# Two score items of the second attention block side by side: four unsplit matmuls in one run on TensorE

## The chip, the core and the metric

The kernel runs on one core of a Trainium2 chip. The metric is device time in microseconds (us) of one execution, as the median of several runs. Before the change three runs gave 736.40, 738.48 and 741.03 us.

## The reference

Attention with a window, then a gated feed-forward. There are 4 batches, 8 heads, 768 positions and 64 dimensions a head. A query sees the 96 positions up to itself (`n_local`) and the first 8 positions (`n_global`); a slope per head times the distance is subtracted from its score.

```
scores = scale * q @ k.T + bias                # bias = -slope[h] * dist
scores = where(is_global | is_local, scores, -1e9)
a = exp(scores - max(scores)); a = a / (sum(a) + 1e-9)
x = (a @ v) reshaped to 3072 x 512
out = (sigmoid(x @ w_gate) * (x @ w_val)) @ w_out   # 512 -> 1536 -> 512
```

Everything is float32.

## The kernel before

**Blocks and units.** The 3072 tokens are cut into 8 blocks of 384 (three tiles of 128). A block's feed-forward is 12 units, one for each slice f of 128 of the 1536 inner features. Unit (block, f) is `ff_in` (L554: 12 matmuls for the gate into bank `ps_g`, 12 for the value into `ps_u`; tanh of the gate on ScalarE, L572; the product on VectorE, L578 or L581) and one unit later `ff_out` (L588: into `ps_o0` to `ps_o2`). Most feed-forward products are made of three matmuls, each on a high or a low part of its two operands ("split").

**Attention of a block** is done in 12 items, (s, t): head pair s of 4, token tile t of 3. For one item:

- `scores` (L359, event "S"): each head of the pair is one matmul with a contraction of 64, on rows 0 to 63 or 64 to 127 of the array. In blocks 0 and 1 (`PAIR` = 1) the float32 operands are used unsplit (L373), head j in bank j; from block 2 on they are split and use the whole array (L387). VectorE then adds the bias table and finds the row minimum of the negated scores (L406), ScalarE takes the exponential (L419). The results go to a buffer of tag `work`, of which there are four; the gate's tanh uses the same tag.
- `normalise` and `transposes` (event "T"): in block 1 VectorE divides by the row sums (L436, L438), TensorE transposes into bank `ps_t` (L452) and ScalarE copies it out (L457).
- `values` (event "V", once per head pair): a @ v into bank `ps_t` (L502), then `pair_out` (L515) splits the result into `xh` (L544) and `xl` (L545), the operands of the next block's `ff_in`.

Block 1's attention runs inside the 12 feed-forward units of block 0. Its scores use two banks, `ps_s` and `ps_v`; each item takes both, so an item's matmuls wait until VectorE has read the item before. Item k of block 1 has its S at unit k*10//12, T and V one unit later.

**Weights.** In the same units the weights are converted from float64 words, slice by slice: DMA on SyncE's queue (`raw`, L175 and L177), ScalarE (L192, L199, and `w1h` at L235), VectorE (L201 to L214), GpSimd (`w1l`, L180). `ff_in` of slice f needs `w1h` and `w1l` of f. From f = 6 on, and in all later blocks, `ff_out` needs `w2h` (ScalarE, L217) and `w2l` (GpSimd, L180).

**Order.** The code gives each unit's events in four groups: 0 ahead of `ff_in`, 1 after its gate matmuls, 2 after `ff_in`, 3 after `ff_out`. This is the order in which instructions are written down, which is their precedence; the framework then simulates the program with its own cost model and lays down, for each engine and for each DMA queue, a fixed order of what it found ready. On the chip each engine goes through its list in that order. `issue_after` adds an edge that fixes an order on an engine.

Of the kernel before, what the change touches and what calls it, by code (L numbers as in the profile page):

```python
# [15 lines left out]
ALU = mybir.AluOpType  # L16
# [3 lines left out]
P = 128  # L20
PREV = 96
GLOB = 32
SLOT = GLOB + P
WIN = PREV + SLOT
# [4 lines left out]
def attn_moe_kernel(ctx, tc, qT, kT, v, n_global, n_local, wg, wv, wo, out, B, H, S, D):  # L29
    nc = tc.nc  # L30
# [28 lines left out]
    wraw = cstack.enter_context(tc.tile_pool(name="wraw", bufs=1))  # L59
    late = {}  # L60

    def issue_after(later, earlier):
        tc.add_manual_dep(
            later.ins,
            earlier.ins.name,
            mybir.DependencyInfo(mybir.DependencyClass.NoSync, mybir.DependencyReason.DATA),
            reason="issue order",
        )

# [22 lines left out]
    last_pe = []  # L92
# [54 lines left out]
    last_min = []  # L147
# [120 lines left out]
    PAIR = 1  # L268
    blocks = [(b, t0, TB) for b in range(B) for t0 in range(0, NTB, TB)]
# [14 lines left out]
    steps = {}  # L284
# [66 lines left out]
    def bank(*names):  # L351

        i = turns.get(names, 0)
        turns[names] = i + 1
        name = names[i % len(names)]
        pool = {"ps_s": ps_a, "ps_t": ps_a, "ps_v": ps_a, "ps_g": ps_gv, "ps_u": ps_gv}.get(name, ps_o)
        return pool.tile([P, 4 * P], F32, name=name)

    def scores(bi, s, t):  # L359
        b, t0, nt = blocks[bi]  # L360
        st = steps[bi, s]
        zero = t0 + t == 0
        w = P if zero else WIN
        qc = slice(t * P, (t + 1) * P)
        k0 = t * SLOT + WIN - w
        if bi <= PAIR:

            ps = [bank(*(("ps_s", "ps_g", "ps_u", "ps_o1") if bi < PAIR else ("ps_s", "ps_v"))) for _ in range(2)]

            lead = None  # L370
            for j in (1, 0):
                hd = slice(j * D, (j + 1) * D)
                ins = nc.tensor.matmul(  # L373
                    ps[j][:, :w], st["qr"][hd, 0, qc], st["kr"][hd, k0:k0 + w], start=True, stop=True
                )
                if lead is not None:
                    issue_after(ins, lead)
                lead = ins
            last_pe[:] = [lead]
            if (bi, s, t) == (0, 0, 1):  # L380
                keep_busy(4)
        else:
            both = bank("ps_s")
            ps = [both[:, j * WIN:(j + 1) * WIN] for j in range(2)]
            for j in range(2):
                for hl in (1, 0):
                    nc.tensor.matmul(  # L387
                        ps[j][:, :w],
                        st["qs"][:, j, hl, qc],
                        st["ks"][:, j, k0:k0 + w],  # L390
                        start=(hl == 1),
                        stop=(hl == 0),
                    )
        build_pair(s, zero, dist)
        sb = mpool.tile([P, 2, WIN], F32, name="work", tag="work", bufs=WORKB)
        i = 2 * ((b * NTB + t0 + t) * NPAIR + s)
        nm = nms[:, i:i + 2]
        if bi < PAIR:
            if t == 0:
                st["sums"] = small.tile([P, 2 * nt], F32, name="sums", bufs=2)  # L400
            sm = st["sums"][:, 2 * t:2 * t + 2]
        else:
            sm = small.tile([P, 2], F32, name="sm")
        for j in range(2):

            ins = nc.vector.tensor_tensor_reduce(  # L406
                sb[:, j, :w],
                ps[j][:, :w],
                (tabs0 if zero else tabs)[2 * s + j],
                -SCALE,  # L410
                3.0e38,
                op0=ALU.add,
                op1=ALU.min,
                accum_out=nm[:, j:j + 1],
            )
            if j and bi <= PAIR:
                issue_after(ins, last_min[-1])
            last_min[:] = [ins]
            ins = nc.scalar.activation(  # L419
                sb[:, j, :w], sb[:, j, :w], AF.Exp, scale=-1.0, bias=nm[:, j:j + 1], accum_out=sm[:, j:j + 1]  # L420
            )
            last_exp[:] = [ins]
        st["s", t] = (sb, sm)
# [91 lines left out]
    def pair_out(bi, s, av, st):  # L515
        b, t0, nt = blocks[bi]
        n = nt * P
        xh, xl = x_of(bi)
        if bi < PAIR:

            sm = st["sums"]
            nc.vector.tensor_scalar(sm, sm, 1e-9, None, op0=ALU.add)
            rc = small.tile([P, 2 * nt], F32, name="rcs", bufs=2)
            nc.vector.reciprocal(rc, sm)
            rows = ps_o.tile([P, 4 * P], F32, name="ps_o2")
            for t in range(nt):
                for j in range(2):
                    nc.tensor.matmul(
                        rows[j * D:(j + 1) * D, t * P:(t + 1) * P],
                        rc[:, 2 * t + j:2 * t + j + 1].to_broadcast([P, D]),  # L530
                        ident,
                        start=True,
                        stop=True,
                    )
            rs = mpool.tile([P, NB], F32, name="hl", tag="hl")
            nc.scalar.copy(rs[:, :n], rows[:, :n])
            x = mpool.tile([P, NB], F32, name="hh", tag="hh")
            nc.vector.tensor_tensor(x[:, :n], av[:, :n], rs[:, :n], op=ALU.mult)
            if s < NPAIR - 1:
                nc.gpsimd.tensor_copy(xh[:, s, :n], x[:, :n])  # L540
                sub(nc.gpsimd, xl[:, s, :n], x[:, :n], xh[:, s, :n])
                return
            av = x
        nc.scalar.activation(xh[:, s, :n], av[:, :n], AF.Copy)  # L544
        nc.vector.tensor_tensor(xl[:, s, :n], av[:, :n], xh[:, s, :n], op=ALU.subtract)  # L545
# [4 lines left out]
    last_out = []  # L550
# [3 lines left out]
    def ff_in(bi, f, mid=None):  # L554
        b, t0, nt = blocks[bi]
        n = nt * P
        xh, xl = x_of(bi)
        pss = []
        for i in range(2):
            ps = ps_gv.tile([P, NB], F32, name=("ps_g", "ps_u")[i])  # L560
            k = 0
            for c in range(NC):
                for wt, xt in ((w1l, xh), (w1h, xl), (w1h, xh)):
                    nc.tensor.matmul(  # L564
                        ps[:, :n], wt[f][:, i, c], xt[:, c, :n], start=(k == 0), stop=(k == 3 * NC - 1)
                    )
                    k += 1
            pss.append(ps)
            if i == 0:
                a = mpool.tile([P, NB], F32, name="work", tag="work", bufs=WORKB)  # L570

                last_gate[:] = [nc.scalar.activation(a[:, :n], ps[:, :n], AF.Tanh, scale=0.5)]  # L572
                if mid is not None:
                    mid()
        if bi < PAIR and f < UNSPLIT:

            h = mpool.tile([P, NB], F32, name="hh", tag="hh")
            nc.vector.scalar_tensor_tensor(h[:, :n], a[:, :n], 1.0, pss[1][:, :n], op0=ALU.add, op1=ALU.mult)  # L578
            hs[bi, f] = (h,)
            return  # L580
        nc.vector.scalar_tensor_tensor(a[:, :n], a[:, :n], 1.0, pss[1][:, :n], op0=ALU.add, op1=ALU.mult)  # L581
        hh = mpool.tile([P, NB], F32R, name="hh", tag="hh")
        hl = mpool.tile([P, NB], F32R, name="hl", tag="hl")
        nc.scalar.activation(hh[:, :n], a[:, :n], AF.Copy)  # L584
        sub(nc.vector, hl[:, :n], a[:, :n], hh[:, :n])
        hs[bi, f] = (hh, hl)
# [45 lines left out]
    events = []  # L632
    for bi, (b, t0, nt) in enumerate(blocks):
        items = [(s, t) for s in range(NPAIR) for t in range(nt)]
        if bi < PAIR:
            w = (-200, -80)
        elif bi == PAIR:
            w = (0, NF - LEAD)
        else:

            w = ((bi - 1) * NF - (LEAD + 1 if bi > PAIR + 1 else 0), bi * NF - LEAD - 1)
        for k, (s, t) in enumerate(items):
            u = w[0] + k * (w[1] - w[0]) // len(items)

            lag = AHEAD if bi < PAIR else 1
            events.append((u, 0, "S", bi, s, t))
            events.append((u + lag, 1, "T", bi, s, t))
            if bi > PAIR:
                events.append((u + 2 * lag, 1, "J", bi, s, t))
            if t == nt - 1:  # L650
                after, kind = (2, 2) if bi < PAIR else (1, 1) if bi == PAIR else (2, 3)
                events.append((u + after * lag, kind, "V", bi, s, t))
    order = sorted(range(len(events)), key=lambda i: (events[i][0], events[i][1], i))
    events = [events[i] for i in order]
# [99 lines left out]
    ps = ps_a.tile([P, 4, P], F32, name="ps_t")  # L754
# [91 lines left out]
    with fits.Else():  # L846
        with tc.For_i(0, B, 1) as b:
            for t0 in range(0, NTB, TB):
                blocks.append((b, t0, TB))
                bi = len(blocks) - 1  # L850
# [45 lines left out]
```

## Time and profile before

| | before |
|---|---|
| median of 3 runs (lowest, highest) | 738.48 us (736.40 to 741.03) |
| the profiled execution: its time, its span | 736.18 us, 734.4 us |
| TensorE matmul busy | 718.1 us, 98% of the span |
| VectorE / ScalarE / GpSimd busy | 498.8 / 420.2 / 219.4 us |
| granted TensorE clock, mean | 0.998 |

Busy time of TensorE counts overlapping matmuls once, and the ends of matmuls are modelled, so what a matmul costs is read from the spacing of starts in the timeline. PE is TensorE's matmuls, DVE VectorE, ACT ScalarE, POOL GpSimd, SPq SyncE's DMA queue. In a timeline row, the brackets say how long the engine was idle before the instruction and what ended that idle time.

### The profile page before, as it was taken

What the parts mean: (1) busy time and instruction counts of PE and PEld (TensorE: products, weight loads), DVE (VectorE), ACT (ScalarE), POOL (GpSimd) and SP (SyncE); (2) the same over time, 40 slices, a digit from 0 to 9 for tenths busy, and PEclk for the clock granted to TensorE, in tenths of its full rate; (3) what the DMA queues carried; (4) which work ended last, traced back from release to release, by engine and by line L of the source; (5) the groups of instructions that cost most, each with busy time, mean ns of one, the idle gap of its engine ahead of it and who ended that gap; (6) DMA issues with size and microseconds to landing.
All of it is one profiled execution on the core that took longest, in us unless ns stands there. A gap on an engine that the chain in (4) does not pass through costs nothing. (4 is left out here: it accounts for less than half of the span.)

```text
span 734.4 us, 12477 instructions
## 1 busy us (share of the span) xinstructions
PE 718.1 (98%) x4403; PEld 653.0 (89%) x4403; DVE 498.8 (68%) x1303; ACT 420.2 (57%) x948; POOL 219.4 (30%) x166
## 2 busy tenths in 40 slices
PE   7999999999999999999999999999999999999996
PEld 5667788999889999999999999999999999999996
DVE  7889799668877777686777868666786877321111
ACT  5789887656565555566456655655555664332222
POOL 5424345422231323223132332313233231221222
PEclk9999999999999999999999999999999999999999
DMA  8969662624437353433435442343435224010001
GB/s 249 275 194 274 189 199 59 167 61 81 106 79 159 85 106 71 100 103 68 79 80 121 110 106 63 65 122 74 96 81 110 72 47 83 16 45 1 1 0 46
DMA packets 136866, 74.27 MB, mean 101 GB/s; under 512 B 87136, under 2 KB 129120, under 8 KB 136800
## 3 DMA queue, kind: packets, MB, share of 16 engines
q1 hardware_dynamic: 136800, 73.43, 40.1%
q8 instruction: 36, 0.59, 0.3%
q14 instruction: 30, 0.25, 0.1%
HBM read 49.81 MB, written 6.29 MB: 76 GB/s over the span
## 5 line engine op out<-in xcount | busy, mean ns | idle before, releaser
L180 POOL TENSOR_TENSOR w2l<-w2f,w2h 128x512 fp32r<-128x512 f32 x89 | 122.5, 1377 | 372.8 <-ACT w2h L217 359.1
L581 DVE SCALAR_TENSOR_TENSOR work<-work,ps_u 128x384 f32<-128x384 f32 x90 | 49.8, 553 | 127.1 <-PE ps_u L564 122.1
L564 PE MATMUL ps_g<-xh,w1l 128*128 128x384 f32 x384 | 131.1, 341 | 1.0 <-ACT work L572 1.0
L564 PE MATMUL ps_u<-xh,w1l 128*128 128x384 f32 x384 | 130.9, 341 | 0.1
L564 PE MATMUL ps_g<-xl,w1h 128*128 128x384 f32 x384 | 129.6, 337 | 0.7 <-DVE xl L545 0.7
L564 PE MATMUL ps_g<-xh,w1h 128*128 128x384 f32 x384 | 129.4, 337 | 0.0
L564 PE MATMUL ps_u<-xh,w1h 128*128 128x384 f32 x384 | 129.3, 337 | 0.0
L564 PE MATMUL ps_u<-xl,w1h 128*128 128x384 f32 x384 | 129.2, 336 | 0.0
L584 ACT ACTIVATE hh<-work 128x384 fp32r<-128x384 f32 x90 | 46.9, 521 | 131.3 <-DVE work L581 131.1
L419 ACT ACTIVATE work<-work,nms 128x256 f32<-128x256 f32 (+1 forms) x192 | 92.0, 481 | 25.8 <-DVE nms L406 25.4
L604 PE MATMUL ps_o<-w2l,hh 128*128 128x512 f32 x267 | 104.9, 393 | 0.6 <-POOL w2l L180 0.5
L604 PE MATMUL ps_o<-w2h,hh 128*128 128x512 f32 x267 | 104.1, 390 | 0.0
L604 PE MATMUL ps_o<-w2h,hl 128*128 128x512 f32 x267 | 103.1, 389 | 0.0
L180 DVE TENSOR_TENSOR hl<-work,hh 128x384 fp32r<-128x384 f32 x90 | 79.6, 884 | 23.4 <-ACT hh L584 23.2
L217 ACT ACTIVATE w2h<-w2f 128x512 fp32r<-128x512 f32 x89 | 56.0, 630 | 52.3 <-PE ps_o L604 51.0
L564 PEld LDWEIGHTS ps_g<-xh,w1l 128*128 128x128 f32 x384 | 72.2, 188 | 5.1 <-issue 2.3
L564 PEld LDWEIGHTS ps_u<-xh,w1l 128*128 128x128 f32 x384 | 72.1, 188 | 3.9 <-issue 1.2
L564 PEld LDWEIGHTS ps_g<-xl,w1h 128*128 128x128 f32 x384 | 72.2, 188 | 2.6 <-DVE xl L545 1.1
L564 PEld LDWEIGHTS ps_u<-xl,w1h 128*128 128x128 f32 x384 | 72.2, 188 | 1.0
L438 DVE TENSOR_SCALAR work<-work,rc 128x256 f32<-128x256 f32 (+1 forms) x168 | 71.4, 464 | 2.0
L564 PEld LDWEIGHTS ps_g<-xh,w1h 128*128 128x128 f32 x384 | 72.2, 188 | 0.5 <-issue 0.2
L564 PEld LDWEIGHTS ps_u<-xh,w1h 128*128 128x128 f32 x384 | 72.2, 188 | 0.0
(133 smaller groups left out, 1170.0 us busy)
## 6 DMA issues: line engine op xcount, KB each, us to landing
qr<-in_qT SPq DMA_DIRECT2D x56, 192.0 KB, 3.3
kr<-in_kT SPq DMA_DIRECT2D x32, 192.0 KB, 2.7
v<-in_v SPq DMA_DIRECT2D x32, 192.0 KB, 3.6
raw<-in_w_gate SPq DMA_DIRECT2D x12, 512.0 KB, 4.3
raw<-in_w_val SPq DMA_DIRECT2D x12, 512.0 KB, 5.6
raw<-in_w_out SPq DMA_DIRECT2D x12, 512.0 KB, 3.8
out<-ost SPq DMA_DIRECT2D x24, 256.0 KB, 2.2
v<-in_v SPq DMA_DIRECT2D x16, 144.0 KB, 3.8
```

What stands on the lines that cost most here:

```text
L180: eng.tensor_tensor(out, a, b, op=ALU.subtract)
L217: ins = nc.scalar.activation(hi, w, AF.Copy)
L419: ins = nc.scalar.activation(sb[:, j, :w], sb[:, j, :w], AF.Exp, scale=-1.0, bias=nm[:, j:j + 1], accum_out=sm[:, j:j + 1])
L438: nc.vector.tensor_scalar(sb[:, j, :w], sb[:, j, :w], rc[:, j:j + 1], None, op0=ALU.mult)
L564: nc.tensor.matmul(ps[:, :n], wt[f][:, i, c], xt[:, c, :n], start=(k == 0), stop=(k == 3 * NC - 1))
L581: nc.vector.scalar_tensor_tensor(a[:, :n], a[:, :n], 1.0, pss[1][:, :n], op0=ALU.add, op1=ALU.mult)
L584: nc.scalar.activation(hh[:, :n], a[:, :n], AF.Copy)
L604: ins = nc.tensor.matmul(outs[bi][t], ht[:, t * P:(t + 1) * P], wt, start=(f == 0 and k == 0), stop=(f == NF - 1 and k == len(parts) - 1),)
```

## The change

For block 1, S events come two items at a time. A new function `pair_scores` writes four matmuls, item k in columns 0 to 255 of the two banks and item k+1 in columns 256 to 511; the second item's S event finds its scores ready. For block 0 it is called with one item and writes what was there before.

```diff
+    def pair_scores(bi, items):
+        names = ("ps_s", "ps_g", "ps_u", "ps_o1") if bi < PAIR else ("ps_s", "ps_v")
+        banks = [bank(*names) for _ in range(2)]
+        free = [] if bi < PAIR else [last_av[-1], last_min[-1]]
+        turn = [] if bi < PAIR else last_out[-1:]
+        with tc.high_priority(offset=0 if bi < PAIR else 400):
+            for i, (s, t) in enumerate(items):
...
+                ps = [b[:, i * WIN:i * WIN + w] for b in banks]
+                for j in (1, 0):
+                    ins = nc.tensor.matmul(ps[j], st["qr"][hd, 0, qc], st["kr"][hd, k0:k0 + w], start=True, stop=True)
+                    for before in free:
+                        issue_after(ins, before, mybir.DependencyClass.Sync)
+                    if bi < PAIR and lead is not None:
+                        issue_after(ins, lead)
+                    for before in turn:
+                        issue_after(ins, before)
...
         if bi <= PAIR:
-            ps = [bank(*(("ps_s", "ps_g", "ps_u", "ps_o1") if bi < PAIR else ("ps_s", "ps_v"))) for _ in range(2)]
-            lead = None
-            for j in (1, 0):
...
+            ps = st.pop(("ps", t), None)
+            if ps is None:
+                ps = pair_scores(bi, [(s, t)])[0] if bi < PAIR else twin_scores(bi, s, t)
...
+            if bi < PAIR:
+                last_out[:] = [ins]        # in ff_in, after the gate's and after the value's matmuls
...
+            if bi == PAIR:
+                at = 4 * (k - k % 2) * w[1] // len(items)
+                turned = at + 4 + 2 * (k % 2)
+                events.append((*divmod(at, 4), "S", bi, s, t))
+                events.append((*divmod(turned, 4), "T", bi, s, t))
+                if t == nt - 1:
+                    events.append((*divmod(turned + 1, 4), "V", bi, s, t))
+                continue
```

The four matmuls wait for the last reader of the two banks (`free`: the last row minimum, and for the first pair the reading of block 0's last `ps_v`), come after the feed-forward matmul written last (`turn`), and have a precedence 400 places higher than their place in the code. Times are counted in quarters of a unit: pairs have their S at quarters 0, 6, 13, 20, 26 and 33 (units 0, 1½, 3¼, 5, 6½, 8¼). The first item's T is one unit later, the second's one and a half, V a quarter after the T of a head pair's last tile. The loads of head pair s+2 are written down with the S of (s, 2), so they move with it.

## Rows read from the trace of the kernel before

**Rows 1.** The page: busy us, share of the span, instructions, for each engine

```profile
PE 718.1 (98%) x4403; PEld 653.0 (89%) x4403; DVE 498.8 (68%) x1303; ACT 420.2 (57%) x948; POOL 219.4 (30%) x166
```

**Rows 2.** Windows: stretch, length, busy PE, PEld, DVE, ACT, POOL; clock; DMA share, GB/s

```profile
41.00:131.00 90.00, 88.48 (x497) 70.00 (x496) 80.31 (x149) 76.05 (x143) 37.23 (x25) 1.00 0.62 189
...
164.00:724.00 560.00, 558.72 (x3418) 524.34 (x3417) 363.50 (x964) 296.72 (x681) 149.47 (x103) 1.00 0.35 77
```

**Rows 3.** Line L373, 33 to 110 us: matmul records, ns minimum/median/maximum, first and last start

```profile
L373 PE MATMUL ps_v<-kr,qr x24: 376/428/480, 36.3 to 107.6; 64*128 64x256 f32 x24
```

**Rows 4.** Timeline of PE (start us, us, instruction): one item of block 1 alone

```profile
38.91 0.34 PE L564 MATMUL ps_u<-xh,w1h 128*128 128x384 f32 x1
39.18 0.48 PE L373 MATMUL ps_v<-kr,qr 64*128 64x256 f32 x1
...
93.61 0.48 PE L373 MATMUL ps_v<-kr,qr 64*128 64x256 f32 x1
...
94.24 0.44 PE L564 MATMUL ps_g<-xh,w1l 128*128 128x384 f32 x1
94.52 0.34 PE L564 MATMUL ps_g<-xl,w1h 128*128 128x384 f32 x1
94.69 0.34 PE L564 MATMUL ps_g<-xh,w1h 128*128 128x384 f32 x1
```

**Rows 5.** Timeline of PE: two items of block 0 back to back, in four banks

```profile
24.53 0.48 PE L373 MATMUL ps_g<-kr,qr 64*128 64x256 f32 x1
...
25.06 0.38 PE L373 MATMUL ps_o<-kr,qr 64*128 64x256 f32 x1
...
25.59 0.87 PE L528 MATMUL ps_o<-ident,rcs 128*64 128x128 f32 x12
```

**Rows 6.** Timeline of PE: its waits around the first items and at the sixth

```profile
38.28 0.44 PE L564 MATMUL ps_g<-xl,w1h 128*128 128x384 f32 x1 [0.74 <-DVE xl L545]
...
40.46 0.42 PE L564 MATMUL ps_g<-xh,w1l 128*128 128x384 f32 x1 [0.57 <-ACT work L572]
...
58.73 0.48 PE L373 MATMUL ps_v<-kr,qr 64*128 64x256 f32 x1 [0.84 <-DVE nms L406]
```

**Rows 7.** Timeline of ACT: an item's first exponential, then the tanh of units 0 and 7

```profile
38.60 0.51 ACT L419 ACTIVATE work<-work,nms 128x256 f32<-128x256 f32 x1 [1.73 <-DVE nms L406]
...
39.84 0.47 ACT L572 ACTIVATE work<-ps_g 128x384 f32<-128x384 f32 x1
...
101.89 0.49 ACT L572 ACTIVATE work<-ps_g 128x384 f32<-128x384 f32 x1
```

**Rows 8.** Timeline of PE: the first gate matmul of units 8 and 10

```profile
102.52 0.41 PE L564 MATMUL ps_g<-xh,w1l 128*128 128x384 f32 x1
...
118.59 0.34 PE L564 MATMUL ps_g<-xh,w1l 128*128 128x384 f32 x1
```

**Rows 9.** Timeline of POOL: both halves of w1l for unit 10

```profile
116.31 2.65 POOL L180 TENSOR_TENSOR w1l<-bits,w1h 128x512 fp32r<-128x512 f32 x2
```

**Rows 10.** Waits, 41 to 131 us: the longest of DVE and of ACT (us, times, longest)

```profile
DVE top L180 <- ACT top L199: 3.0, 5, 1.0
...
ACT w1h L235 <- DVE bits L212: 6.8, 5, 2.3
```

**Rows 11.** Timeline of PE and of DVE: block 2's first item, both heads in one bank

```profile
134.02 0.56 PE L387 MATMUL ps_s<-ks,qs 128*128 128x128 f32 x4
...
134.62 0.29 DVE L406 CUSTOM_DVE_ANT_0 work<-ps_s,tabs 128x128 f32<-128x128 f32 x1 [0.65 <-PE ps_s L387]
```

**Rows 12.** Timeline of PE: an item of block 0 whose heads were parted

```profile
12.26 0.59 PE L373 MATMUL ps_o<-kr,qr 64*128 64x256 f32 x2
...
13.14 0.70 PE L373 MATMUL ps_u<-kr,qr 64*128 64x256 f32 x2
```

**Rows 13.** Timelines of SPq and ACT: a load of raw and the conversion that reads it

```profile
66.78 0.43 SPq L175 DMA_DIRECT2D raw<-in_w_val  x1
...
78.93 1.11 ACT L192 ACTIVATE bits<-raw 128x1024 int32<-128x1024 uint32 x1
```

More of the change, by code (lines that the diff above doesn't have):

```diff
@@ L60, in attn_moe_kernel, with issue_after @@
     late = {}
-    def issue_after(later, earlier):
+    def issue_after(later, earlier, kind=mybir.DependencyClass.NoSync):
         tc.add_manual_dep(
@@ L65, in issue_after @@
             earlier.ins.name,
-            mybir.DependencyInfo(mybir.DependencyClass.NoSync, mybir.DependencyReason.DATA),
+            mybir.DependencyInfo(kind, mybir.DependencyReason.DATA),
             reason="issue order",
@@ L357, in bank, with twin_scores @@
         return pool.tile([P, 4 * P], F32, name=name)
+    last_av = []
+    def pair_scores(bi, items):
[3 more added lines that the diff above has]
+        turn = [] if bi < PAIR else last_out[-1:]
+        lead = None
+        out = []
+        with tc.high_priority(offset=0 if bi < PAIR else 400):
+            for i, (s, t) in enumerate(items):
+                st = steps[bi, s]
+                w = P if blocks[bi][1] + t == 0 else WIN
+                qc = slice(t * P, (t + 1) * P)
+                k0 = t * SLOT + WIN - w
+                ps = [b[:, i * WIN:i * WIN + w] for b in banks]
+                for j in (1, 0):
+                    hd = slice(j * D, (j + 1) * D)
+                    ins = nc.tensor.matmul(ps[j], st["qr"][hd, 0, qc], st["kr"][hd, k0:k0 + w], start=True, stop=True)
[5 more added lines that the diff above has]
+                        issue_after(ins, before)
+                    lead = ins
+                out.append(ps)
+        last_pe[:] = [lead]
+        return out
+    def twin_scores(bi, s, t):
+        nt = blocks[bi][2]
+        s2, t2 = divmod(s * nt + t + 1, nt)
+        ps, steps[bi, s2]["ps", t2] = pair_scores(bi, [(s, t), (s2, t2)])
+        return ps
     def scores(bi, s, t):
@@ L366, in scores @@
         if bi <= PAIR:
-            ps = [bank(*(("ps_s", "ps_g", "ps_u", "ps_o1") if bi < PAIR else ("ps_s", "ps_v"))) for _ in range(2)]
-            lead = None
-            for j in (1, 0):
[L372 to L379, printed above, removed]
+            ps = st.pop(("ps", t), None)
+            if ps is None:
+                ps = pair_scores(bi, [(s, t)])[0] if bi < PAIR else twin_scores(bi, s, t)
             if (bi, s, t) == (0, 0, 1):
@@ L537, in pair_out @@
             x = mpool.tile([P, NB], F32, name="hh", tag="hh")
[L538 removed]
+            last_av[:] = [nc.vector.tensor_tensor(x[:, :n], av[:, :n], rs[:, :n], op=ALU.mult)]
             if s < NPAIR - 1:
@@ L563, in ff_in @@
                 for wt, xt in ((w1l, xh), (w1h, xl), (w1h, xh)):
-                    nc.tensor.matmul(
+                    ins = nc.tensor.matmul(
                         ps[:, :n], wt[f][:, i, c], xt[:, c, :n], start=(k == 0), stop=(k == 3 * NC - 1)
@@ L650, in attn_moe_kernel @@
             if t == nt - 1:
-                after, kind = (2, 2) if bi < PAIR else (1, 1) if bi == PAIR else (2, 3)
+                after, kind = (2, 2) if bi < PAIR else (2, 3)
                 events.append((u + after * lag, kind, "V", bi, s, t))
```

## The prediction, made before the changed kernel was run

> **What bounds the kernel now.** I read the page first: TensorE has matmuls in flight for 98% of the span [rows 1], so any other engine matters only where TensorE waits for it. The table of windows says where that is. From 164 to 724 us TensorE is busy for 558.72 of 560 us [rows 2]: this long part takes what TensorE's own work takes, and begins earlier if block 0's units end earlier. All the work that the change touches lies before it, between 36.3 and 107.6 us, where the 12 items of block 1 show as 24 records in each of two banks, two records for each float32 matmul [rows 3]. From 41 to 131 us TensorE idles for 1.5 of 90 us. VectorE has 80.3 us of work there and ScalarE 76.1, much of it weight conversion [rows 2]. The waits of these two engines are for each other, the longest ScalarE's 6.8 us for VectorE's `bits` and VectorE's 3.0 us for ScalarE's `top` [rows 10]; in this stretch the waits list has none of the two for TensorE. So here two things run at nearly the same speed: TensorE, and the conversion that gives it its weights. The reader should keep both in mind: what TensorE saves is kept only as far as the conversion lets it run ahead.
>
> **The change, part by part.** *Fewer changes between half-array and whole-array matmuls.* First what an item alone costs. Feed-forward matmuls start 0.17 us apart (94.52, 94.69). The item at 39.18 starts 0.27 us after its predecessor, 0.10 too late. From its start to the next matmul it takes 0.63 us (93.61 to 94.24), and the one after that comes 0.28 us later, 0.11 too late [rows 4]. Together 0.10 + 0.63 + 0.11 = 0.84 us. Two items back to back are in the trace too, in block 0: from 24.53 to 25.59, 1.06 us for both [rows 5], so the second adds 0.43 us and no change of its own. A pair then costs 0.10 + 1.06 + 0.11 = 1.27 us instead of 1.68, and saves 0.41. Six pairs: 2.46 us. The rows of block 0 use four banks and the change uses two, with the items in the two halves of each. The bounds for this unknown are 0.41 a pair (as in four banks) and 0 (each item still pays 0.84); I take 0.41, because in either layout the two heads of an item go to different banks and each bank just gets a second run of columns.
>
> *The first pair* gains nothing that lasts. TensorE waits 0.74 us for `xl` right after item 0 and 0.57 us for ScalarE's tanh right after item 1 [rows 6]; the second item now fills the first of these gaps, and what it leaves goes into the second, since that tanh comes at 39.84 whatever TensorE does with item 1 [rows 7]. So five pairs count: 5 x 0.41 = 2.05 us.
>
> *The wait at 58.73* goes. There TensorE waited 0.84 us for the row minima of item 4 before it could start item 5 [rows 6]. These two are a pair now. The next pair comes 1½ to 1¾ units later, 13 us or so (units 8 and 10 start 16.07 us apart [rows 8], about 8 us each), and its predecessor's four row minima should be long done. The gross gain is 2.05 + 0.84 = 2.9 us.
>
> *What is late next.* A TensorE that is early has to be given its operands early. Two hand-overs are close. ScalarE's tanh of unit 7, which frees `ps_g`, ends at 102.38, and unit 8's first gate matmul comes at 102.52, 0.14 us later [rows 7, 8]. GpSimd makes `w1l` for unit 10 in two halves from 116.31, so the first is there at about 116.31 + 2.65/2 = 117.6 (estimate from that row), and unit 10 starts at 118.59: 1.0 us to spare [rows 8, 9]. The tanh can move, because its place in ScalarE's list is chosen anew. The `w1l` stands at the end of the whole conversion, through which nothing in the change passes faster. Both ends for what is kept: nothing (the tanh binds as it stands) and all 2.9 us (every list shifts along). I take 1.0 us, the slack of `w1l`, after the last pair of block 1; behind unit 10 no scores of block 1 are left to gain more.
>
> *The second item's work on VectorE and ScalarE* is not more, only closer together: four row minima and four exponentials in a run. From an item's first exponential to the tanh behind it ScalarE takes 1.2 us (38.60 to 39.84) [rows 7]. I cost it at nothing, since the four minima have the next 13 us; if that cover is gone, it is the slow rival below. In a bank that two items share, the first item's minimum also has to wait for the second item's matmuls. Block 2 has this case: its four matmuls into one bank run from 134.02 for 0.56 us, and an idle VectorE begins at 134.62, behind all four, though the first head was done after two [rows 11]. Here that is 0.43 us on VectorE, six times, and VectorE has 9.7 us idle in the stretch [rows 2].
>
> The Trainium skill ("PSUM — Partial Sum Buffer", PSUM bank collisions) says to guard a bank, not an address, because a reader and a writing matmul on different columns of one bank still collide. The trace agrees at 134.62. By that rule, with VectorE taken as the bound of the whole stretch, six times 0.43 us would come off the gain of 2.9 and leave 0.3.
>
> *The waits added.* Each of the four matmuls waits for the preceding pair's last minimum; behind them in TensorE's list stand feed-forward matmuls, for which everything downstream waits. Bounds: 0, and the 0.84 us seen once before the change, at each of five pairs, 4.2 us. I take 0 by the 13 us spacing.
>
> *The loads that move.* The queries, keys and values of head pair s+2 are written down with S of (s, 2), which shifts by at most half a unit or so, and V, which frees the value buffers, by half a unit later for s = 0 and 2. SyncE's queue is in order, so the `raw` loads behind a value load could wait 4 us longer. A `raw` load issued at 66.78 is read at 78.93, 12 us later [rows 13], which covers it; without that cover each of these two delays could cost up to 4 us. Earlier S and V for the last head pair help block 1's first unit, if at all.
>
> *Sum.* 736.18 us for the profiled execution, minus 1.0, is 735.2. The median of the runs, 738.48, stands 2.3 above that execution; the forecast on the median is 738.48 - 1.0 = **737.5 us**.
>
> **The rivals.** *A: everything is kept.* ScalarE's and VectorE's lists shift along, as the place of the tanh allows. For it: 9.7 and 14 us idle on the two [rows 2]; against it: they idle for one another, not for TensorE [rows 10]. 738.48 - 2.9 = 735.6 us.
>
> *B: the pair doesn't stay together.* Inside block 1 the edge that kept an item's second head behind its first is no longer written, and precedence alone holds the four matmuls in a row. Block 0 shows a case in which other work came between the heads: 0.59 us for one and 0.70 for the other, no longer side by side [rows 12], 1.29 us where 0.63 would do. If half of the pairs break up between the items there is little gain, and each parted item costs 0.66 us; two gone wrong cancel the 1.0. 738.5 us. For it: the order comes from a simulation; against it: the four have one precedence and the same waits.
>
> *C: slower, by ScalarE's list.* Both items' exponentials stand ahead of a gate's tanh, 1.2 us more in front of it, and the tanh holds `ps_g` and so the next unit. It decides wherever the tanh has less than 1.2 us to spare, as in unit 7 with 0.14 us. At all six pairs: 6 x 1.2 - 2.05 = 5.2 us more, 743.7; at half of them 3.6 - 2.05 = 1.6 more, 740.1. For it: rows 7 and 8; against it: the tanh of unit 0 shows that the simulation does place it right behind one item, so it can place it between two.
>
> **How the numbers follow.** Forecast (0.4 to 2 us gained) 0.42; A 0.25; B 0.15; C 0.18. The runs before reach 2.1 below and 2.6 above their median. Low: A's 735.6 minus most of 2.1, 733.5; high: C at half its places 740.1 plus half of 2.6, 741.4. The range is 733.5 to 741.5, and leaves out C in full and a deeper A. One per cent, 7.4 us, is about what a measurement of this kernel tells from no change. Faster by more than that is out of reach of these steps: the five pairs' 2.05 us and every wait of TensorE in block 0's units, 1.5 us from 41 to 131 us [rows 2] and 1.3 us around the first items [rows 6], make 4.9 us: 0.02. Slower by more needs C in full with late value loads: 0.04. Within 1%: 0.94.
>
> **What would show it right or wrong.** In the timeline six runs of eight records of the score matmuls, about 1.06 us from first start to the next whole-array matmul, and no other work between: parted runs mean B. The wait for `nms` gone from TensorE's list. The first gate matmul of unit 10 not before `w1l` for it: if it comes 2 us or more earlier than 118.59 with no wait, A holds. Idle time of TensorE in front of `ps_g` with ScalarE's L572 as its end, once a pair, is C. From 164 us on, the same spacing as before; if TensorE's work there has changed, the forecast is wrong for a reason that none of these steps names.

## The result, and the profile after

Over six runs each, the changed kernel takes 748.81 us (median) and the kernel before 739.5 (its first three runs are those of the table before): ratio 1.0147, 95% interval 1.012 to 1.0174. (One run of the changed kernel took 2510 us and is left out of the ratio.) It is slower by about 1.5%, where I had forecast 737.5 us, within 733.5 to 741.5. The profiled execution of after took 751.06 us, with a span of 749.2 and a mean granted clock of 0.988; before it was 736.18, 734.4 and 0.998.

The page of the kernel after, busy time by engine (columns as in [rows 1]):

```profile
PE 726.3 (97%) x4403; PEld 661.1 (88%) x4403; DVE 499.1 (67%) x1303; ACT 420.7 (56%) x948; POOL 217.8 (29%) x166
```

VectorE, ScalarE and GpSimd have the work they had in [rows 1], to within 1.6 us; the instruction counts are equal. Nothing was added. TensorE is busy 8.2 us longer with the same matmuls, and the span is 14.8 us longer.

Windows of after (columns as in [rows 2]):

```profile
41.00:131.00 90.00, 82.02 (x443) 65.14 (x442) 69.80 (x141) 72.32 (x135) 30.55 (x22) 0.94 0.55 181
164.00:300.00 136.00, 131.86 (x796) 122.63 (x795) 104.47 (x274) 77.54 (x183) 39.18 (x25) 0.97 0.44 92
164.00:724.00 560.00, 555.86 (x3387) 521.06 (x3386) 371.45 (x982) 297.55 (x685) 148.22 (x100) 0.99 0.35 77
```

From 41 to 131 us TensorE now idles 8.0 of 90 us instead of 1.5 [rows 2]. VectorE is busy 69.8 us there instead of 80.3, and ScalarE and GpSimd less too: all four engines got through less work in the same time, as engines do that wait for one another. From 164 to 300 us TensorE idles 4.1 us. And the granted clock, 1.00 in both of before's rows, is 0.94 and 0.97.

**The pairs do what I said.** Timeline of TensorE after, the second pair from the matmul in front of it to the one behind:

```profile
43.86 0.34 PE L591 MATMUL ps_u<-xh,w1h 128*128 128x384 f32 x1
44.12 0.48 PE L378 MATMUL ps_v<-kr,qr 64*128 64x256 f32 x1
...
44.88 0.38 PE L378 MATMUL ps_v<-kr,qr 64*128 64x256 f32 x1
...
45.19 2.84 PE L633 MATMUL ps_o<-w2f,hh 128*128 128x512 f32 x6
```

Eight records in one run, from 44.12 to 45.19: 1.07 us for two items, as block 0's 1.06 [rows 5]. All six pairs are whole, starting at 36.31, 44.12, 64.03, 74.50, 98.10 and 108.55.

**The waits have changed hands.** TensorE's waits after, 41 to 131 us (us in total, times, longest):

```profile
PE ps_o L633 <- POOL w2l L180: 3.2, 1, 3.2
PE ps_g L591 <- POOL w1l L180: 2.4, 2, 1.9
PE ps_t L479 <- ACT pT L484: 1.2, 1, 1.2
PE ps_t L529 <- ACT pT L484: 0.8, 1, 0.8
```

The wait for `nms` at 58.73 [rows 6] is gone, and no wait stands before a pair. In its place are converted weights that come late (5.6 us) and softmax results that come late (2.0 us).

Timeline of TensorE after, first gate matmul of units 8 and 10, as [rows 8]:

```profile
106.28 0.42 PE L591 MATMUL ps_g<-xh,w1l 128*128 128x384 f32 x1
...
128.01 0.43 PE L591 MATMUL ps_g<-xh,w1l 128*128 128x384 f32 x1
```

Unit 8 is 3.8 us later than before and unit 10 is 9.4 later. Unit 4 was still early (67.67 against 68.59).

Timeline of GpSimd after: `w1l` for unit 10, as [rows 9], and for unit 11:

```profile
123.78 2.62 POOL L180 TENSOR_TENSOR w1l<-bits,w1h 128x512 fp32r<-128x512 f32 x2 [0.36 <-ACT w1h L235]
133.60 3.43 POOL L180 TENSOR_TENSOR w1l<-bits,w1h 128x512 fp32r<-128x512 f32 x2 [2.40 <-ACT w1h L235]
```

The conversion reaches unit 10 at 123.78, against 116.31 [rows 9], and unit 11 at 133.60, against 122.12. I had said of this `w1l` that nothing in the change makes it earlier; I had not asked what makes it later. VectorE's two longest waits after, 41 to 131 us, as [rows 10]:

```profile
DVE top L180 <- ACT top L199: 7.7, 6, 3.2
DVE top L180 <- ACT neg L199: 6.0, 2, 3.1
```

VectorE waits 13.7 us for ScalarE in these two; its longest was 3.0 in [rows 10]. One case shows how. Timeline of ScalarE after, around the third pair:

```profile
66.40 0.51 ACT L446 ACTIVATE work<-work,nms 128x256 f32<-128x256 f32 x1
...
67.89 0.49 ACT L446 ACTIVATE work<-work,nms 128x256 f32<-128x256 f32 x1
...
68.39 1.11 ACT L192 ACTIVATE bits<-raw 128x1024 int32<-128x1024 uint32 x1
69.41 1.10 ACT L199 ACTIVATE top<-raw 128x1024 int16<-128x1024 int16 x1
70.42 1.10 ACT L199 ACTIVATE neg<-raw 128x1024 int16<-128x1024 int16 x1
```

Both items' exponentials stand in one run, the conversion behind them, and VectorE's subtraction of `neg` begins at 71.55 after 3.06 us idle (the fifth of its kind; before, it began at 66.87).

**The clock.** Windows of after (columns as in [rows 2], the clock is the third number from the end):

```profile
86.00:92.40 6.40, 5.61 (x14) 4.68 (x15) 4.49 (x6) 5.13 (x9) 2.27 (x3) 0.50 0.53 188
123.40:126.60 3.20, 3.12 (x7) 2.48 (x8) 3.20 (x4) 1.45 (x2) 2.64 (x3) 0.50 0.43 123
174.80:181.30 6.50, 5.71 (x18) 5.20 (x18) 4.26 (x8) 2.13 (x6) 1.73 (x2) 0.50 0.39 83
```

In these three stretches TensorE was granted 1.2 GHz instead of 2.4, so by my estimate half of its busy time there is lost: (5.61 + 3.12 + 5.71) / 2 = 7.2 us. The timeline of TensorE after shows the waits at the first two:

```profile
84.22 0.66 PE L479 MATMUL ps_t<-ident,work 128*128 128x128 f32 x4 [1.21 <-ACT pT L484]
...
86.79 0.69 PE L591 MATMUL ps_g<-xh,w1l 128*128 128x384 f32 x1 [1.92 <-POOL w1l L180]
...
123.48 0.80 PE L633 MATMUL ps_o<-w2l,hh 128*128 128x512 f32 x1 [3.16 <-POOL w2l L180]
```

**The sum.** Up to 131 us: 6.5 us more idle, 4.4 of clock, less 2.5 for the pairs, 8.4 worked out. Block 1's first `ff_out` begins its `w2l` matmuls at 155.74 against 146.27, 9.5 later; some 1.1 us I can't assign. From 164 to 300: 2.9 us more idle (4.14 against 136 - 134.72 = 1.28) and 2.9 of clock, 5.7 worked out; the lateness has grown from 9.5 to 14.9 by the 54th `w2l` matmul (245.36 against 230.47). From there to the end nothing is added.

### The profile page after: what moved, and what is told of

Same layout as the page of the kernel before. It is cut to its first block, busy times and chain, and to the rows that moved or that the text cites. A ratio compares the mean times of both kernels' runs of the same rounds, so it can differ in the third digit from the quotient of the medians.

```text
span 749.2 us, 12481 instructions
## 1 busy us (share of the span) xinstructions
PE 726.3 (97%) x4403; PEld 661.1 (88%) x4403; DVE 499.1 (67%) x1303; ACT 420.7 (56%) x948; POOL 217.8 (29%) x166
## 5 line engine op out<-in xcount | busy, mean ns | idle before, releaser
L591 PE MATMUL ps_g<-xh,w1l 128*128 128x384 f32 x384 | 132.7, 345 | 5.2 <-POOL w1l L180 2.9
L591 PE MATMUL ps_u<-xh,w1l 128*128 128x384 f32 x384 | 132.5, 345 | 0.9 <-DVE work L610 0.8
L180 DVE TENSOR_TENSOR hl<-work,hh 128x384 fp32r<-128x384 f32 x90 | 77.1, 857 | 25.0 <-ACT hh L613 24.9
L494 DVE COPY halves<-work 128x512 int16<-128x512 int16 (+1 forms) x144 | 62.6, 477 | 18.2 <-DMA turned<-halves 16.7
```

The costliest lines, as they stand in the source:

```text
L180: eng.tensor_tensor(out, a, b, op=ALU.subtract)
L494: nc.vector.tensor_copy(dst, words[:, :, :, h])
L591: ins = nc.tensor.matmul(ps[:, :n], wt[f][:, i, c], xt[:, c, :n], start=(k == 0), stop=(k == 3 * NC - 1))
```

## The experiments

Ratios are against runs of the kernel before on the same chip, measured beside each experiment, whose medians were 736.1 to 737.5 us. Of each experiment one execution was traced. My first theory was that the second item's softmax, bunched behind the first, delays the conversion on ScalarE and VectorE; the rivals were the new edges, the precedence, and the new event times by themselves.

### Which part of the change costs it

**times_only**: the kernel before, single items, and only the new event times.

```diff
+            if bi == PAIR:
+                at = 4 * (k - k % 2) * w[1] // len(items)
+                turned = at + 4 + 2 * (k % 2)
...
+                continue
```

> The kernel before with only the new event times for block 1 (S of two items in one place, T and V as in the change); each item still has its own two matmuls on TensorE, no precedence and no added waits. Theory 1, bunching: both items' minima and exponentials now stand in a row in VectorE's and ScalarE's lists, ahead of the weight conversion, and that makes the loss: 745 to 750 us, the last w1l of block 0 about 10 us later than before. Theory 2, TensorE's side (the precedence of 400 places, or the added waits and edges): nothing of that is here, so 737 to 741 us. Theory 3, chance of the planner's order: any rewriting moves the time by several us, anything from 736 to 750.

Measured 749.0 us, 1.0172 [1.015, 1.0195]. Without one pair it is as slow as the whole change.

**pair_old_times**: the change with the old event times.

```diff
-            if bi == PAIR:
...
-                after, kind = (2, 2) if bi < PAIR else (2, 3)
+                after, kind = (2, 2) if bi < PAIR else (1, 1) if bi == PAIR else (2, 3)
```

> The changed kernel with the old event times of block 1: the four matmuls of a pair go together with the precedence and the added waits, but the second item's minima and exponentials are written down where they were. Theory 1, bunching: back to about 736 to 739 us. Theory 2, TensorE's side: stays at 745 to 750 us. Theory 3, chance: anything from 736 to 750.

Measured 742.63 us, 1.0099 [1.0066, 1.0131]: 6.6 us, about half of what the change without its precedence or its edges loses (no_prec and no_edges, below). Timeline of TensorE in this kernel, first gate matmul of units 5 and 10:

```profile
73.80 0.42 PE L591 MATMUL ps_g<-xh,w1l 128*128 128x384 f32 x1
...
120.29 0.52 PE L591 MATMUL ps_g<-xh,w1l 128*128 128x384 f32 x1
```

Unit 5 comes 2.8 us earlier than before (76.61). That is close to my gross gain of 2.9, but in part by luck, since it is another sum: only four pairs have run by then, the first of them counts too (4 x 0.41 = 1.6), and from 33 us on TensorE has idled 1.4 us instead of 2.7. By unit 10 the gain has turned into a loss of 1.7 (118.59 in [rows 8]), at 171.73 (the 28th `w2l` matmul) the loss is 4.3, and from 215 us on 6.25.

**no_prec** and **no_edges**: the change without the precedence, and without the new edges.

```diff
-        with tc.high_priority(offset=0 if bi < PAIR else 400):
+        with tc.high_priority(offset=0):
```

> The changed kernel with the precedence of the pair's matmuls set from 400 places to 0; times, pairs and edges as in the change. Theory 1, bunching: stays at 745 to 750 us. Theory 2, if it is the precedence: 736 to 740 us. Theory 3, chance: anything from 736 to 750.

```diff
-                    for before in free:
-                        issue_after(ins, before, mybir.DependencyClass.Sync)
-                    if bi < PAIR and lead is not None:
+                    if lead is not None:
                         issue_after(ins, lead)
-                    for before in turn:
-                        issue_after(ins, before)
```

> The changed kernel without the added edges (no wait of the pair for the preceding pair's last minimum beyond what the banks need, no place behind the feed-forward matmul written last; the second matmul issues behind the first as before). Theory 1, bunching: stays at 745 to 750 us. Theory 2, if it is the edges: 736 to 740 us. Theory 3, chance: anything from 736 to 750.

Measured 749.52 us, 1.0192 [1.0153, 1.0231], and 749.03, 1.0166 [1.0148, 1.0184]. Both are as slow as the change: neither part matters here.

### Is it the conversion's edges to the softmax?

The conversion's first instructions carry edges behind the last exponential or minimum written down, which after the change is the second item's. **firstitem_after** points them at the pair's first item; **unpin_after**, **unpin_before** and **unpin_pairold** (on pair_old_times) drop them from the first unit on.

```diff
-        if last_exp:
-            issue_after(first, last_exp[-1])
+        if pin_exp:
+            issue_after(first, pin_exp[-1])
```

> The changed kernel with one difference: the two edges in conv_a, which put each conversion's first ScalarE instruction behind the exponential written last and its first VectorE instruction behind the row minimum written last, point in block 1 to the first item of a pair only. Theory 1a, the conversion is held behind two items by these edges: most of the loss goes, 737 to 742 us, and ScalarE's list shows conversions between the first and the second item's exponentials. Theory 1b, bunching by precedence alone, the edges don't matter: 746 to 750 us. Theory 3, chance of the order: anything from 736 to 750.

```diff
-        if last_exp:
+        if last_exp and not loose:
...
-            if last_min:
+            if last_min and not loose:
```

> The changed kernel without the two edges of conv_a from block 0's first unit on. Theory 1a: 736 to 742 us, the last w1l at most 3 us later than before. Theory 1b: 746 to 750 us. Theory 3: anything from 736 to 750.

> The kernel before without the two edges of conv_a from block 0's first unit on, as a control for the run above. Theory 1a: one item's exponentials were not much in the way, so 735 to 739 us, near the kernel before. Theory 3: the order is as good as drawn anew, 736 to 750 us.

> The changed kernel with the old event times of block 1 and without the two edges of conv_a. With the pairs' gain on TensorE (2 us or so by the first units of the run with old times) and the conversion free, theory 1a: 734 to 739 us, below the 742.6 us of the run with old times. Theory 1b: 741 to 744 us. Theory 3: anything from 736 to 750.

Measured: firstitem_after 747.31 us, 1.0122 [1.0081, 1.0163]; unpin_after 750.05, 1.0164 [1.0135, 1.0193]; unpin_before 748.5, 1.0153 [1.0122, 1.0183]; unpin_pairold 748.34, 1.0138 [1.0111, 1.0165]. The unpinned conversion does run earlier: its last `w1l` comes at 115.17 in unpin_after, against 122.12 before and 133.60 after. It helps nothing, since now softmax results are late. TensorE's longest waits, 41 to 131 us, first in unpin_after, then in unpin_before:

```profile
PE ps_t L480 <- ACT pT L485: 5.5, 1, 5.5
PE ps_g L592 <- ACT work L602: 2.3, 1, 2.3
```

```profile
PE ps_v L374 <- DVE nms L407: 3.3, 3, 2.1
PE ps_t L453 <- DVE xl L546: 1.8, 1, 1.8
```

So a late `w1l` is not the cause by itself: weights and softmax share two engines, and here one came forward and the other fell back. The three runs without edges also changed more than was meant: they lose 7.4, 3.8 and 6.0 us ahead of block 0's units already (at the last row-sum matmul of block 0's attention, L528, which before starts at 31.72). firstitem_after loses nothing there (0.03 us early) and is still as slow as the change within the intervals, and that is what speaks against this theory.

### Is it the bunching, or any new order?

**after_spread** keeps the pairs but puts the second item's softmax half a unit later. **shift_S** is a neutral control: the kernel before, no pair, no bunching, S of block 1 written down after the unit's gate matmuls instead of ahead of them.

```diff
-                events.append((*divmod(at, 4), "S", bi, s, t))
+                events.append((*divmod(at + 2 * (k % 2), 4), "S", bi, s, t))
```

> The changed kernel with the second item of each pair having its S event (minima and exponentials; its matmuls stay in the pair) two quarters of a unit after the first item's; T and V as in the change. Theory 1, the loss comes from two items' minima and exponentials in a row: 736 to 741 us. Theory 3, every other order than the one of the kernel before loses some 5 to 12 us of its balance: 742 to 750 us.

```diff
-            events.append((u, 0, "S", bi, s, t))
+            events.append((u, 1 if bi == PAIR else 0, "S", bi, s, t))
```

> The kernel before with one small, neutral difference: the S events of block 1 stand after the gate matmuls of their unit instead of ahead of them. No pairs, no bunching, single items as before. Theory 1, bunching: 735 to 740 us. Theory 3, every other order loses: 742 to 750 us.

Measured 746.56 us, 1.0111 [1.0078, 1.0144], for after_spread: 0.0036 lower than the change's ratio, with overlapping intervals, so bunching isn't shown to be more than a small part. (Its trace is 2.8 us late ahead of block 0's units, after a stretch of half clock that after's doesn't have.) And 751.18 us, 1.0181 [1.0146, 1.0216], for shift_S: a shift that pairs nothing and removes nothing costs as much as the change. Windows of shift_S:

```profile
41.00:131.00 90.00, 82.57 (x453) 63.62 (x453) 68.92 (x142) 73.28 (x140) 32.05 (x22) 0.99 0.55 175
164.00:300.00 136.00, 131.06 (x809) 121.91 (x808) 105.12 (x282) 77.70 (x184) 39.06 (x25) 1.00 0.43 95
```

and TensorE's longest waits in it, 41 to 131 us:

```profile
PE ps_g L564 <- POOL w1l L180: 3.5, 3, 1.5
PE ps_o L604 <- DVE hh L578: 2.2, 2, 1.7
PE ps_t L452 <- ACT pT L457: 1.2, 1, 1.2
```

The same picture as after the change: 7.4 us idle, VectorE at 68.9 us, and waits for weights, for a product and for softmax results. The clock is hardly lower here (0.99, 1.00), so it makes the loss larger but isn't needed for one.

### Is it that the engines have no room?

**light_before** and **light_after** leave out the conversion's `top` and `neg` instructions (L199, L201 and on, and the addition into the top halves), so the weights lack a term; everything else is there.

```diff
-        c["top"] = top = wraw.tile([P, 2 * CW], I16, name="top", bufs=TOPB)[:, 0:n]
...
-            nc.vector.scalar_tensor_tensor(top, c.pop("top"), 8.0, top, op0=ALU.mult, op1=ALU.add)
+        return
```

> The kernel before with most of the weight conversion left out (of each slice only ScalarE's first instruction, w1h, w1l, w2h and w2l stay; the instructions on top and neg are gone, so the weights are not the reference's). TensorE's own work is unchanged. It is the control for light_after. If block 0's units are at the limit of TensorE alone, 733 to 737 us; if the conversion costs TensorE more than its waits show, clearly less.

> The changed kernel with the same part of the weight conversion left out as in light_before. Theory 4, ScalarE and VectorE have no room in block 0's units: with room made, the pairs' gain on TensorE is kept, 1.5 to 3.5 us less than light_before. Rival, the pairs or the new times cost TensorE something by themselves: as slow against light_before as the change is against before, 5 to 11 us more.

Measured 736.72 us, 0.9988 [0.9968, 1.0008], and 731.03, 0.9923 [0.9897, 0.995]. With the conversion light, the change makes the kernel faster, by 5.7 us, more than the 1.5 to 3.5 that I expected. Windows of light_after, then of light_before:

```profile
41.00:131.00 90.00, 90.00 (x535) 74.47 (x534) 32.44 (x108) 56.47 (x125) 34.01 (x26) 1.00 0.59 198
```

```profile
41.00:131.00 90.00, 90.00 (x520) 71.88 (x517) 30.30 (x106) 57.77 (x126) 33.86 (x26) 1.00 0.62 197
```

TensorE never idles in either. The last row-sum matmul of block 0's attention comes at 31.19 in light_after and 30.68 in light_before, 0.5 us later; block 0's last `ff_out` begins at 133.84 and 135.83, 2.0 earlier. So block 0's units gain 2.5 us, and 2.46 is what I had worked out for six pairs: that part of the working holds once the other engines can follow. The other 4.0 us arise behind it, where light_before idles more (5.4 us from 131 to 300, against 2.4). There light_before also loses the 2.7 us by which block 0's last `ff_out` comes earlier than in the kernel before (138.51), so its time, equal to before's, doesn't say that the conversion costs block 0 nothing.

**actroom_after** leaves out one of ScalarE's two conversion activations (the subtraction then yields zero), **dveroom_after** VectorE's addition of `top` into the weights, both in the changed kernel and for the slices converted that way.

```diff
-            for dst, sign in ((top, 1.0), (neg, -1.0)):
-                ins = nc.scalar.activation(dst, w3, AF.Relu, scale=8.0 * sign, bias=-8.0 * 14336.0)
-                issue_after(ins, first)
-            sub(nc.vector, top, top, neg)
+            ins = nc.scalar.activation(top, w3, AF.Relu, scale=8.0, bias=-8.0 * 14336.0)
+            issue_after(ins, first)
+            sub(nc.vector, top, top, top)
```

> The changed kernel with one instruction of ScalarE left out per slice of w_gate and w_val (neg, 1.13 us each, 11 slices; VectorE subtracts top from itself instead, so the weights are not the reference's). If ScalarE is the engine without room: 733 to 739 us. If VectorE is: 744 to 750 us. If both bind in turn: 739 to 744 us.

```diff
-            nc.vector.tensor_tensor(top, c.pop("top"), top, op=ALU.add)
+            return
```

> The changed kernel with one instruction of VectorE left out per slice of w_gate and w_val (the addition into bits, 1.31 us each, 11 slices, so the weights are not the reference's); ScalarE has all its work. If VectorE is the engine without room: 733 to 739 us. If ScalarE is: 744 to 750 us. If both bind in turn: 739 to 744 us.

Measured 747.58 us, 1.0145 [1.0123, 1.0166], and 743.1, 1.0084 [1.0068, 1.0101]. By their pages ScalarE has 11.1 us less to do (420.7 to 409.6) and VectorE 13.9 (499.1 to 485.2). On the whole time ScalarE's room gives back nothing that can be measured (the change stood at 1.0147); VectorE's gives back 0.0063, about 4.6 us. Windows of actroom_after, then of dveroom_after:

```profile
41.00:131.00 90.00, 82.72 (x468) 65.52 (x467) 76.48 (x154) 64.70 (x133) 33.15 (x22) 1.00 0.58 183
```

```profile
41.00:131.00 90.00, 84.78 (x489) 68.82 (x486) 65.67 (x147) 76.40 (x146) 35.51 (x24) 1.00 0.61 190
```

This points to VectorE, but doesn't show that it is the engine without room. 743.1 lies in the range expected if both bind in turn (739 to 744), not in that for VectorE (733 to 739). Each of the two is also a new order, and after_spread and pair_old_times, which give no engine room, take 0.0036 and 0.0048 off the change's ratio. And in both traces the granted clock is 0.50 from 11.5 to 20.5 us, where after's is 1.00, so that they are 2.9 and 2.7 us late ahead of block 0's units. Counted from there to unit 10's first gate matmul (128.01 in after, 127.43 and 121.47 here), after loses 9.4 us, actroom_after 5.9 and dveroom_after 0.2; but no_prec, with no room added, loses 5.4. If VectorE is the tighter engine, busy time doesn't tell: in after's own row it idles longer than ScalarE.

### Versions that might keep the gain

**pooln_pairold** and **pooln_before** move block 1's division by the row sums from VectorE to GpSimd, on pair_old_times and on the kernel before. **one_pair_6** and **one_pair_10** pair only items 6 and 7, or 10 and 11, with old times and without the new edges and precedence.

```diff
-            nc.vector.tensor_scalar(sb[:, j, :w], sb[:, j, :w], rc[:, j:j + 1], None, op0=ALU.mult)
+            (nc.gpsimd if bi == PAIR else nc.vector).tensor_scalar(sb[:, j, :w], sb[:, j, :w], rc[:, j:j + 1], None, op0=ALU.mult)
```

> The changed kernel with the old event times of block 1, and with block 1's division by the row sums on GpSimd instead of VectorE (24 instructions, 0.3 us each on VectorE); the results are the reference's. If VectorE's lack of room is what takes the pairs' gain: 733 to 738 us, below the kernel before. If GpSimd's slower division comes late for the transposes, or the order matters more than the room: 740 to 750 us.

> The kernel before with block 1's division by the row sums on GpSimd, the control for pooln_pairold. If room on VectorE were all that mattered: 734 to 738 us. If any other order than the one of the kernel before loses: 742 to 750 us.

```diff
-                ps = pair_scores(bi, [(s, t)])[0] if bi < PAIR else twin_scores(bi, s, t)
+                ps = twin_scores(bi, s, t) if bi == PAIR and s * nt + t in (6,) else pair_scores(bi, [(s, t)])[0]
```

> The kernel before with one pair only, items 6 and 7, whose S events stand in the same place already; no new times, no precedence, no added edges. If the pair's own gain is all that comes of it: 0.4 us less than before, not to be told from no change. If every other order than the one of the kernel before loses: 739 to 748 us.

> The kernel before with one pair only, items 10 and 11, the last two; item 11's S event stays one unit later. If the pair's own gain is all that comes of it: 0.4 us less than before, not to be told from no change. If every other order loses, less of it is left to change here than with items 6 and 7: 737 to 742 us.

Measured: pooln_pairold 743.08 us, 1.0088 [1.0071, 1.0105]; pooln_before 746.13, 1.0136 [1.0118, 1.0154]; one_pair_6 743.13, 1.0079 [1.0054, 1.0103]; one_pair_10 741.72, 1.005 [1.0025, 1.0074]. None with all the work in it beats the kernel before, and even one pair, worth 0.41 us on TensorE, costs 4 to 6.

Not all of that is a new order. In one_pair_10 TensorE, VectorE, ScalarE and SyncE's queue go through the same lists as before up to 104 us, and GpSimd throughout; yet unit 4 begins at 71.58 instead of 68.59, 3.0 us late. Timelines of VectorE and GpSimd before, just ahead of the minima for which TensorE waits at 58.73:

```profile
56.28 1.71 DVE L438 TENSOR_SCALAR work<-work,rc 128x256 f32<-128x256 f32 x2
56.54 2.58 POOL L180 TENSOR_TENSOR w1l<-bits,w1h 128x512 fp32r<-128x512 f32 x2 [3.97 <-ACT w1h L235]
```

In one_pair_10, with TensorE's next score matmul, and its windows:

```profile
56.79 2.65 DVE L461 TENSOR_SCALAR work<-work,rc 128x256 f32<-128x256 f32 x2
56.50 2.78 POOL L180 TENSOR_TENSOR w1l<-bits,w1h 128x512 fp32r<-128x512 f32 x2 [3.49 <-ACT w1h L235]
60.18 0.48 PE L378 MATMUL ps_v<-kr,qr 64*128 64x256 f32 x1 [1.87 <-DVE nms L429]
...
61.50:64.70 3.20, 3.20 (x14) 2.76 (x14) 3.17 (x9) 2.24 (x4) 1.07 (x1) 0.50 0.89 276
```

Before, the first of VectorE's two scalings took 0.34 us and was all but done when GpSimd began; here GpSimd began first, and both took about 1.4 us. TensorE's wait, 0.84 us at 58.73 [rows 6], became 1.87, and half clock followed. It was 0.4 us late ahead of that wait, 1.45 behind it and 3.0 behind the stretch at half clock. The trace of one_pair_6 shows the same (scalings 2.65 us, a wait of 1.85). So an overlap that shifts by half a microsecond was followed by 3 us of delay with no instruction in another place so far. Whether before's own slower executions (up to 741.0 us) do this isn't shown; only one of them has a trace.

## Why the prediction was wrong

**What held.** A pair costs TensorE what I worked out, no pair was parted (rival B did not happen), the wait at 58.73 went, and no pair waits. In block 0's units of light_after the saving is the one worked out for six pairs.

**A smaller miss.** The first pair was to gain nothing that lasts, "since that tanh comes at 39.84 whatever TensorE does with item 1". Timelines of ScalarE and TensorE after, the tanh of unit 0 and unit 1's first gate matmul behind it:

```profile
39.18 0.47 ACT L601 ACTIVATE work<-ps_g 128x384 f32<-128x384 f32 x1
39.79 0.41 PE L591 MATMUL ps_g<-xh,w1l 128*128 128x384 f32 x1 [0.47 <-ACT work L601]
```

The tanh moved ahead of three of the pair's four exponentials, and unit 1 begins 0.67 us earlier than before (40.46 in [rows 6]).

**The step that failed** is the sizing of what is kept: "Both ends for what is kept: nothing (the tanh binds as it stands) and all 2.9 us (every list shifts along)". The low end should have been a loss. Two terms stood at nothing and fed it. "The loads that move" took from the new event times only the loads; times_only, which has those times alone, loses 749.0 - 736.1 = 12.9 us. The second is what pairing itself does to the other engines' lists. It has no term of its own but rival B; pair_old_times, which pairs and leaves the softmax events where they were, loses 6.6 us. (The term that I did name and "cost ... at nothing", the second item's minima and exponentials close behind the first's, isn't shown to be large: after_spread.) The two do not add up, since the whole change loses 9.3 to 13.5 us (this result, and no_prec and no_edges, which differ from it by parts without effect).

**Why.** [rows 10] showed VectorE and ScalarE waiting for each other and not for TensorE, and I read this as slack on both. The runs speak for the opposite: with 80.3 and 76.1 us of work in 90 [rows 2], strung on hand-overs between them, they just kept up. The four other orders that I tried with no pair in them (times_only, shift_S, unpin_before, pooln_before) lose 10 to 15 us, whatever was moved. With the conversion light, the same change wins. So the cause is shown as far as this: the hand-overs that feed TensorE in block 0's units, and in part just behind them, have no reserve, and edits that pair nothing, or one pair of items, lose 4 to 15 us in all; with most of the conversion gone the pairs gain in block 0's units what I worked out. Two ways into the loss are seen: another order of the lists, and, in one_pair_10, the order of before with one overlap shifted and the clock that falls with the wait. How the loss of the change divides between them, and whether VectorE above all has too little room, is argued and not shown.

**The rivals.** C was nearest, in that the loss comes through ScalarE's and VectorE's lists, but it put the place at the gate's tanh, which in unit 0 came forward, and the price at 5.2 us at most; TensorE's waits are for `w1l`, `w2l` and `pT`, and the clock came on top. I gave slower by over 1% a chance of 0.04, since I asked only what each moved step pushes behind itself and not what a new order of everything would do.

**What I listed as telling.** "From 164 us on, the same spacing as before" failed as well, and as said there for a reason outside my steps: TensorE waits there for block 1's products and for block 2's preparation. TensorE's waits after, 164 to 300 us (before it had only 1.2 us for `ks`):

```profile
PE ps_g L591 <- ACT work L601: 1.8, 1, 1.8
PE ps_s L414 <- DVE ks L180: 1.1, 1, 1.1
PE ps_u L591 <- DVE work L610: 0.8, 1, 0.8
```

**What stays open.** Which moved instruction costs which part of it isn't settled; nor why pair_old_times, 2.8 us early at unit 5, loses it again; nor whether before's order is one of few good ones, since only the orders above were run. A pair within before's order of the other engines, held by edges, was not tried, nor more `work` buffers.

## What to carry to other kernels

Where two engines that feed the bound one are busy for 80 to 90% of a stretch and wait for each other, don't take their idle time for slack: ask what removing work from *them* would give before taking work from the bound engine. Where a scheduler lays down all lists anew, every edit is also a new order; a neutral shift of the same events (here shift_S, +14.8 us) shows the size of that term, and it belongs in the range on both sides. Before laying a loss to the new order, look where the lists first differ: in one_pair_10 the loss began ahead of that. A saving of 2.5 us can't be told from a term of 10 by reasoning about the saved instructions alone.

## What the runs showed of the hardware

When after's granted clock first fell to 0.50, between 85.7 and 85.8 us, TensorE had waited 1.21 us, worked for 0.65 (86.79 - 1.92 - 84.22) and stood about 0.9 us into a wait that became 1.92. It stayed at 1.2 GHz until 92.4, with TensorE busy for 5.61 of the last 6.40 us. In one_pair_10 it fell about 1.3 us behind a single wait of 1.87 us. Before, single waits of 0.84 us and less in this part [rows 6] cost no clock. I had priced waits at their own length; here 7.2 us of half speed stand beside 9.4 us of added waits.

VectorE's scaling of an item pair's four tiles took 1.14 us in one place and 3.19 in another. Timeline of VectorE after:

```profile
44.04 1.14 DVE L465 TENSOR_SCALAR work<-work,rc 128x256 f32<-128x256 f32 x4
...
50.20 3.19 DVE L465 TENSOR_SCALAR work<-work,rc 128x256 f32<-128x256 f32 x4
```

and of GpSimd:

```profile
50.62 2.61 POOL L180 TENSOR_TENSOR w1l<-bits,w1h 128x512 fp32r<-128x512 f32 x2 [11.18 <-ACT w1h L235]
```

GpSimd worked on `w1l` through most of the slow one and was idle in the other (it idled for 11.18 us up to 50.62). So a shift changes not only when VectorE's instructions stand but how long they take. In one_pair_10 this is seen at the start of a loss. What part it has in the change's own loss I did not isolate: pooln_pairold, which takes this scaling off VectorE, gained nothing over pair_old_times (743.08 against 742.63).
